# A scan with a gated feed-forward on one core: an earlier load of h, and the first two down products exchanged

## The chip, the cores and the metric

The kernel runs on one core of a Trainium2 chip. The time is the device time of one execution in microseconds (us), the median over several runs. One more execution was taken with the hardware profiler; its views (waits, timelines, windows) are what the prediction reads. The engines of a core are called by short names: PE is TensorE (matrix products, with its weight loads as PEld), DVE is VectorE, ACT is ScalarE, POOL is GpSimd, and SP issues most DMA transfers. Each engine works through its own list of instructions in the order in which the program gives them; an instruction that waits holds back all that stand behind it on the same engine.

## The reference

```python
def reference(A_x, A_wqkv, A_wo, B_x, B_w_gate, B_w_up, B_w_down):
    ...
    x = A_x
    xn = _layernorm(x, axis=-1)
    s = _A_ref(xn, A_wqkv, A_wo)
    g = _silu(_B_ref(xn, B_w_gate, B_w_up, B_w_down))
    return x + s * g
```

`x` has 2048 rows of 640. `_A_ref` is attention of 32 heads over 8 earlier rows, each two apart, with a product by `wo` (640 x 640) at its end. `_B_ref` is `((x W_gate) * (x W_up)) W_down`, with 1536 columns in the middle. All is float32.

## The kernel before

**The whole.** The 2048 rows make 16 tiles of 128. The kernel has three stages for TensorE: the products with `wqkv`, `w_gate` and `w_up`, beside the attention on the other engines; then the output product with `wo` for pairs of tiles (`pair_product`, L981); then the down product with `w_down` for pairs of tiles (`product`, L853). The middle result h (the gated product) and the attention's output go through DRAM: `h_scr` holds h, tile by tile, and `s_scr` the output of `wo`.

**Float32 in two parts.** Every operand of a matmul is split into a high part (a copy to the type fp32r, on ACT) and a low part (the operand less its high part, on DVE or POOL), and each product is three: high by high, high by low, low by high, in this order. So an operand costs one ACT instruction and one DVE or POOL instruction before TensorE can use it. For h these are `hi_h(m)` (L820, ACT at L822) and `lo_h(m)` (L824, DVE at L826); for a pair of the `wo` stage `hi_pair` and `lo_pair` (L968, L972); for weights `split_wd` (L781), whose helper `split` (L112) runs ACT at L114 and POOL at L115.

**Seven products for a pair.** A pair of tiles, seen as a 2 x 2 matrix of blocks A11 to A22, is multiplied with the 2 x 2 blocks of the weight in seven block products instead of eight, by sums of blocks. The seven left operands are, in order, A11, S1, S2, S4, S3, A12 and A22 (`H_IN`, L731), and the right ones B11, T1, T2, B22, T3, B21 and T4 (`W_IN`). For h the sums are made by `sum_h` (L803) on DVE: S1 = A21 - A22 (L810), S2 = S1 - A11 (L812), S4 = A12 + S2 (L815), S3 = A11 - A21 (L818; it is written in the place of A21). S1 needs the second tile of the pair alone, S2 needs S1 and the first tile.

**Banks.** The products add into three PSUM banks, and which product uses which is the string `"ACACABA"` (L856): product 0 starts bank A, product 1 bank C, product 2 adds into A, product 3 into C, product 4 into A, product 5 starts bank B, product 6 adds into A. `gather(m)` (L866) follows each product. For product 0 it is `keep("M1")`, for product 1 `keep("M5")`, for product 2 `keep("U2")`: a copy of the bank by ACT (L840), which must be done before the next product adds into that bank.

**The border.** The loop over pairs p = 0 to 7 (L1490) makes the seven products of pair p, and between them prepares pair p + 1; the first product of pair p + 1 stands before the last product of pair p. In its last rounds it prepares the down stage too, all in an order written out by hand:

- at the start of p = 6, `load_h(0, (1,))` loads the second tile of h's first pair (768 KB, L795 on SP); after product 4 of p = 6, `load_h(0, (0,))` loads the first. Each takes the buffer (tag `t`, two buffers) of an earlier pair of the `wo` stage and waits for `lo_pair` of that pair;
- in p = 7, `sum_h(1)` (S1) stands after product 1, `hi_h(1)`, `lo_h(1)` and `hi_h(0)` after product 2, `lo_h(0)` after product 4, and `sum_h(2)` (S2) after product 5;
- behind the loop stand two splits of T4 weights, the loads for later (`load_h(1)`, `load_sx`), then `hi_h(2)`, `sum_h(3)` (S4) and `lo_h(2)`.

In the copies of a pair's products, ACT at L999 and L1010 and DVE at L1002 to L1007, TensorE's banks are read; L1010 is the copy after product 6.

**The down stage.** Its loop over m runs four products ahead (`AHEAD`): behind product m and `gather(m)` stand `hi_h(m + 4)` on ACT, then the sum for m + 5 and `lo_h(m + 4)` on DVE. At m = 0 there stand first `hi_h(3)`, `sum_h(4)` (S3) and `lo_h(3)`. So on ACT the order is: the copy of the first product, `hi_h(3)`, `hi_h(4)`, the copy of the second product, and so on; `hi_h(4)` needs S3.

Of the kernel before, what the change touches and what calls it, by code (L numbers as in the profile page):

```python
# [42 lines left out]
NP = NT // 2  # L43
# [13 lines left out]
def kernel(  # L57
# [70 lines left out]
    def slot(shape, dt=F32R):  # L128
        return st(shape, "s", SLOTS, dt)
# [651 lines left out]
    def split_wd(u):  # L781

        n = sum(len(ks) for _, ks in u)
        y, r = w_row[u[0][0], u[0][1][0]]
        split(nc.gpsimd, wd_raw.pop(u), *(y[:, r:r + n, l] for l in range(2)))
# [3 lines left out]
    def load_h(n, rows=(0, 1)):  # L789

        v = h_raw.setdefault(n, {})
        if n % 2 == 0:
            for i in rows:
                t = st([P, KF, P], "t", 2)
                nc.sync.dma_start(t, h_scr[2 * n + i])  # L795
                v.update({f"A{i + 1}1": t[:, :KH], f"A{i + 1}2": t[:, KH:]})
        else:
            for name, i, k, tag, m in (("A11", 0, 0, "wraw", 2), ("A21", 1, 0, "s", SLOTS), ("A12", 0, KH, "o", 1),
                                       ("A22", 1, KH, "wraw", 2)):
                v[name] = st([P, KH, P], tag, m)  # L800
                nc.sync.dma_start(v[name], h_scr[2 * n + i][:, k:k + KH])

    def sum_h(m):  # L803

        n, name = m // 7, H_IN[m % 7]
        v = h_raw[n]
        if name == "S1":
            y = slot([P, 2, KH, P], F32)
            v["S1"], v["S2"] = y[:, 0], y[:, 1]
            nc.vector.tensor_sub(v["S1"], v["A21"], v["A22"])  # L810
        elif name == "S2":
            nc.vector.tensor_sub(v["S2"], v["S1"], v["A11"])  # L812
        elif name == "S4":
            v["S4"] = slot([P, KH, P], F32)
            nc.vector.tensor_add(v["S4"], v["A12"], v["S2"])  # L815
        elif name == "S3":
            v["S3"] = v["A21"]
            nc.vector.tensor_sub(v["S3"], v["A11"], v["A21"])  # L818

    def hi_h(m):  # L820
        hT[m] = slot([P, 2, KH, P])
        nc.scalar.activation(hT[m][:, 0], h_raw[m // 7][H_IN[m % 7]], AF.Copy)  # L822

    def lo_h(m):  # L824
        n, name = m // 7, H_IN[m % 7]
        nc.vector.tensor_sub(hT[m][:, 1], h_raw[n][name], hT[m][:, 0].bitcast(F32))  # L826
        if name == "A22" and n + 2 < NT // 2:
            load_h(n + 2)
# [24 lines left out]
    def product(m):  # L853
        j = m % 7
        name = W_IN[j]
        place = "ACACABA"[j]  # L856
        new = j in (0, 1, 5)
        if new:
            bank[place] = pt([P, HALF], {"A": "q", "B": "g", "C": "u"}[place], {"A": 3, "B": 2, "C": 2}[place])
        p, y = bank[place], hT.pop(m)  # L860
        runs = [(i, l, k) for i, l in ((0, 0), (0, 1), (1, 0)) for k in range(KH)]
        for r, (i, l, k) in enumerate(runs):
            nc.tensor.matmul(p, y[:, i, k], wd_part(name, k, l), start=new and r == 0, stop=r == len(runs) - 1,  # L863
                             skip_group_check=True)

    def gather(m):  # L866

        n, j = divmod(m, 7)
        a, b = 2 * n, 2 * n + 1
        p = bank["ACACABA"[j]]  # L870
        if j == 0:
            keep("M1", p, "lg", 2)
        elif j == 1:
            keep("M5", p, "lg", 2)
        elif j == 2:
            keep("U2", p, "gh", 5)
        elif j == 3:
            g_t[a] = slot([P, D], F32)
            nc.vector.tensor_sub(g_t[a][:, HALF:], p, kept["U2"])
            return lambda: silu(a, 1)  # L880
        elif j == 4:
            g_t[b] = slot([P, D], F32)
            nc.vector.tensor_sub(g_t[b][:, HALF:], kept["M5"], p)
            return lambda: silu(b, 1)
        elif j == 5:
            nc.vector.tensor_add(g_t[a][:, :HALF], kept["M1"], p)
            return lambda: silu(a, 0)
        else:
            return lambda: silu(b, 0, p)
        return lambda: None  # L890
# [90 lines left out]
    def pair_product(p, j):  # L981
        place = "ACACABA"[j]
        new = j in (0, 1, 5)
        if new:
            bank[p, place] = pt([P, HALF], {"A": "q", "B": "g", "C": "u"}[place], {"A": 3, "B": 2, "C": 2}[place])
        b = bank[p, place]
        runs = [(pair_in(p, H_IN[j], k, i), w_part(W_IN[j], k, l)) for i, l in ALL3 for k in range(KS)]
        if j in FIFTH:
            name, c = FIFTH[j]
            runs += [(pair_in(p, name, 0, i), wo_t["W0-W1"][:, l] if c is None else wo_s[KD - 1][l][:, c:c + HALF])  # L990
                     for i, l in ALL3]
        for r, (y, w) in enumerate(runs):
            nc.tensor.matmul(b, y, w, start=new and r == 0, stop=r == len(runs) - 1, skip_group_check=True)  # L993
        if j == 0:
            pair_first[p] = st([P, HALF], "lg", 2)
        kept = [pair_first[p]] + [pair_k[0][:, i] for i in range(2)]
        ya, yb = y_t.setdefault((p, "y"), [None, None])
        if j < 3:
            nc.scalar.activation(kept[j], b, AF.Copy)  # L999
        elif j == 3:  # L1000
            ya = y_t[p, "y"][0] = st([P, D], "gh", 5)
            nc.vector.tensor_add(ya[:, HALF:], kept[2], b)  # L1002
        elif j == 4:
            yb = y_t[p, "y"][1] = st([P, D], "gh", 5)
            nc.vector.tensor_add(yb[:, HALF:], kept[1], b)
        elif j == 5:
            nc.vector.tensor_add(ya[:, :HALF], kept[0], b)  # L1007
            nc.sync.dma_start(s_scr[2 * p], ya)
        else:
            nc.scalar.activation(yb[:, :HALF], b, AF.Copy)  # L1010
            nc.sync.dma_start(s_scr[2 * p + 1], yb)
# [339 lines left out]
    for m, t in ((m, t) for m in range(1, len(MADE)) for t in range(DIL)):  # L1351
# [3 lines left out]
        for i in range(NE):  # L1355
            n = t * NE + i
# [92 lines left out]
    def unit(name, *ks):  # L1449
        return ((name, ks),)  # L1450
# [32 lines left out]
    def low_then_split(p, part, n):  # L1483
        lo_pair(p, part)
        behind(pair_z[p, part][0][1][:, KD - 1, P - 1:].bitcast(F32))
        split_next(n)
# [3 lines left out]
    for p in range(NP):  # L1490
        more = p + 1 < NP
        if p:
            wd_loads()
        if p == NP - 2:
            load_h(0, (1,))
        elif not more:
            load_wd((unit("T3", 4, 5), unit("T4", 2, 3)), "pk", 1)
            load_wd((unit("T4", 4, 5),), "gh", 5)
        pair_product(p, 1)
        if more:  # L1500
            hi_pair(p + 1, 0)
            low_then_split(p + 1, 0, 1)
        else:
            split_next()
            sum_h(1)
        pair_product(p, 2)
        if more:
            hi_pair(p + 1, 2)
        else:
            hi_h(1)  # L1510
            lo_h(1)
            hi_h(0)
        pair_product(p, 3)
        if more:
            hi_pair(p + 1, 1)
        else:
            split_next(2)
        pair_product(p, 4)
        if more:
            lo_pair(p + 1, 2)  # L1520
            if p == NP - 2:
                load_h(0, (0,))
        else:
            lo_h(0)
        pair_product(p, 5)
        if not more:
            sum_h(2)
            split_wd(unit("T3", 4, 5))
        if more:
            low_then_split(p + 1, 1, 2 if p in (5, 6) else 1)  # L1530
        if p == 0:
            load_pair(4)
        elif p > 1 and p + 3 < NP:
            load_pair(p + 3)
        if p + 2 < NP:
            turn_pair(p + 2)
        if more:
            pair_product(p + 1, 0)
        pair_product(p, 6)
    split_wd(unit("T4", 4, 5))  # L1540
    split_wd(unit("T4", 2, 3))
    load_h(1)
# [5 lines left out]
    lo_h(2)  # L1548
    for m in range(n_prod):
        n, j = divmod(m, 7)  # L1550
        product(m)
        after = gather(m)
        if m == 0:
            hi_h(AHEAD - 1)
            sum_h(AHEAD)
            lo_h(AHEAD - 1)
        if m + AHEAD < n_prod:
            hi_h(m + AHEAD)
        after()
        if m + AHEAD + 1 < n_prod:  # L1560
            sum_h(m + AHEAD + 1)
        if m + AHEAD < n_prod:
            lo_h(m + AHEAD)
        if j < 2 and n:
            gated(2 * n - 2 + j)
            load_sx(2 * n + j)
        if m == n_prod - 3:
            gated(NT - 2, HALF)
            gated(NT - 1, HALF)
        elif m == n_prod - 2:  # L1570
            gated(NT - 2, 0)
# [44 lines left out]
```

## Time and profile before

| | |
|---|---|
| Median of 3 runs | 742.34 us (741.77 to 743.74) |
| The profiled execution, its own time | 741.97 us |
| Its span, from the first to the last event of the core | 740.1 us |
| Down stage, its first product's start | 586.03 us from the start of the span |
| Mean granted TensorE clock | 0.999 |

A row of a timeline gives the start and the length in us, the engine, the line of the kernel, the operation, the tiles it writes and reads (without buffer numbers), the shapes, and a count where several instructions in a row are merged. In square brackets stands the idle time of the engine just before it and what ended that. In a row of waits the three numbers are the total, how often, and the longest. The tiles of this border: `t` are h's two tiles of the first pair and the pairs' raw data, `s` are operands and sums, `q`, `e`, `u` and `g` are PSUM banks (bank A is a `q` or an `e`, bank C is a `u`, bank B is a `g`), `lg` is where `keep` copies the first two products to, `xc` and `kv` hold split weights, and `wraw`, `pk` and `gh` hold weights as they were loaded.

### The profile page before, as it was taken

Reading aid. Unit: us, or ns where it says so; the run is one execution under the profiler, and the core shown is the slowest. Engines: PE = TensorE matmul, PEld = TensorE weight load, DVE = VectorE, ACT = ScalarE, POOL = GpSimd, SP = SyncE. Lnnn points to the kernel's source line nnn. Section 1 sums busy time; section 2 is a strip of 40 time slices with the busy share of each in tenths; the row PEclk is TensorE's granted clock in tenths of the full one; section 3 lists DMA queues with packets and bytes.
Section 4 is the critical chain, followed back from the end, with each engine's and each line's share of the span. In section 5 each row is a group of like instructions: output and inputs, shape, how many; then the busy total and the mean of one; then the engine's idle time right before and its main releaser. Section 6 shows DMA issues by size and latency. Waiting matters only on the chain.

```text
span 740.1 us, 11057 instructions
## 1 busy us (share of the span) xinstructions
PE 730.8 (99%) x4030; PEld 665.4 (90%) x4030; DVE 625.9 (85%) x729; ACT 301.4 (41%) x560; POOL 448.4 (61%) x382
## 2 busy tenths in 40 slices
PE   8999999999999999999999999999999999999997
PEld 6989989988999998887878888888999999999997
DVE  7676998799786989899989999968888887777775
ACT  5668312323232333233323332335556654444442
POOL 6159929997788889797879969577543720000000
PEclk9999999999999999999999999999999999999999
DMA  9465588889767659452634443268667855555534
GB/s 331 160 203 166 218 281 301 249 255 256 190 183 190 228 163 362 120 188 60 205 92 118 158 141 91 74 199 224 204 213 231 305 203 192 192 192 193 193 107 142
DMA packets 106292, 143.78 MB, mean 194 GB/s; under 512 B 23064, under 2 KB 75284, under 8 KB 106238
## 3 DMA queue, kind: packets, MB, share of 16 engines
q1 hardware_dynamic: 88510, 121.13, 51.3%
q10 hardware_dynamic: 16000, 12.78, 5.4%
q0 software_dynamic: 1728, 9.18, 5.3%
q8 instruction: 31, 0.51, 0.3%
q14 instruction: 23, 0.19, 0.1%
HBM read 94.40 MB, written 55.67 MB: 203 GB/s over the span
## 4 chain that ended last, share of the span: by engine, by line
PE 92%; POOL 2%; DVE 2%; issue 2%; DMA 1%; ACT 1%; SPq 0%; POOLq 0%; DVEq 0%; ACTq 0%
PE g L1289 14%; PE q L434 10%; PE u L1289 9%; PE u L434 8%; PE q L863 8%; PE g L434 8%; PE u L863 5%; PE g L124 5%; PE u L124 5%; PE q L1289 4%; PE q L993 3%; PE e L863 3%; PE g L863 3%; PE u L993 2%; PE e L434 1%
## 5 line engine op out<-in xcount | busy, mean ns | idle before, releaser
L514 POOL TENSOR_TENSOR o<-o,t 128x960 f32<-128x960 f32 (+1 forms) x66 | 132.9, 2014 | 9.5 <-DVE t L508 8.5
L508 DVE TENSOR_TENSOR t<-e,kv 128x960 f32<-128x960 f32 (+1 forms) x96 | 99.6, 1038 | 16.7 <-POOL o L514 16.7
L542 DVE TENSOR_TENSOR t<-q,kv 128x1920 f32<-128x1920 f32 (+1 forms) x48 | 92.5, 1926 | 2.9 <-DMA kv<-qkv_scr 1.9
L549 DVE TENSOR_REDUCE lg<-t 128x96 f32<-128x1920 f32 (+1 forms) x48 | 92.3, 1923 | 0.2
L434 PE MATMUL q<-s,xc 128*128 128x360 f32 (+1 forms) x450 | 82.9, 334 | 0.2 <-POOL s L115 0.2
L1258 ACT ACTIVATE gh<-g 128x512 f32<-128x512 f32 x57 | 34.1, 599 | 113.1 <-PE g L1289 109.4
L115 POOL TENSOR_TENSOR s<-wraw,s 128x384 fp32r<-128x384 f32 (+6 forms) x57 | 69.5, 1231 | 17.6 <-ACT s L114 17.6
L434 PEld LDWEIGHTS q<-s,xc 128*128 128x128 f32 x450 | 74.8, 188 | 4.3 <-POOL s L115 1.3
L434 PE MATMUL u<-s,xc 128*128 128x360 f32 (+1 forms) x360 | 65.8, 334 | 0.0
L434 PEld LDWEIGHTS u<-s,xc 128*128 128x128 f32 x360 | 60.3, 188 | 2.3
L434 PE MATMUL g<-s,xc 128*128 128x360 f32 (+1 forms) x330 | 61.5, 337 | 0.0
L1289 PE MATMUL u<-xc,s 128*128 128x512 f32 x228 | 58.1, 390 | 0.3 <-POOL s L115 0.3
L1289 PE MATMUL g<-s,s 128*128 128x512 f32 x228 | 58.0, 390 | 0.2 <-ACT gh L1258 0.2
L434 PEld LDWEIGHTS g<-s,xc 128*128 128x128 f32 x330 | 55.7, 188 | 2.6
L863 PE MATMUL q<-xc,s 128*128 128x320 f32 x342 | 55.5, 309 | 0.0
L863 PEld LDWEIGHTS q<-xc,s 128*128 128x128 f32 x342 | 51.5, 188 | 0.0
L1289 PEld LDWEIGHTS u<-xc,s 128*128 128x128 f32 x228 | 42.8, 188 | 9.6 <-POOL s L115 0.8
L1289 PEld LDWEIGHTS g<-s,s 128*128 128x128 f32 x228 | 42.7, 188 | 9.5 <-ACT gh L1258 0.6
L114 ACT ACTIVATE s<-wraw 128x384 fp32r<-128x384 f32 (+6 forms) x58 | 32.6, 581 | 29.8 <-PE g L1289 10.2
L1289 PE MATMUL g<-xc,s 128*128 128x512 f32 x171 | 42.0, 390 | 0.1
L1289 PE MATMUL q<-xc,pk 128*128 128x512 f32 x171 | 41.9, 389 | 0.0
L826 DVE TENSOR_TENSOR s<-s,s 128x768 fp32r<-128x768 f32 x28 | 30.5, 1088 | 11.8 <-ACT s L822 11.8
(332 smaller groups left out, 1547.0 us busy)
## 6 DMA issues: line engine op xcount, KB each, us to landing
h_scr<-gh SPq DMA_DIRECT2D x48, 256.0 KB, 2.6
wraw<-in_wgu SPq DMA_DIRECT2D x11, 640.0 KB, 4.4
kv<-qkv_scr SPq DMA_DIRECT2D x14, 480.0 KB, 6.0
t<-h_scr SPq DMA_DIRECT2D x8, 768.0 KB, 5.9
qkv_scr<-s ACTq DMA_DIRECT2D x17, 360.0 KB, 4.3
kv<-qkv_scr SPq DMA_DIRECT2D x14, 367.5 KB, 6.8
s_scr<-gh SPq DMA_DIRECT2D x16, 320.0 KB, 3.3
gh<-s_scr SPq DMA_DIRECT2D x16, 320.0 KB, 4.1
```

Source lines behind the costliest of these rows:

```text
L114: nc.scalar.activation(hi, raw, AF.Copy)
L115: eng.tensor_sub(lo, raw, hi.bitcast(F32))
L124: nc.tensor.matmul(acc, a, b, start=first and n == 0, stop=last and n == len(runs) - 1)
L434: nc.tensor.matmul(p, xT[(r * NE + i) // TPC][a][:, k, t0:t0 + P], wq[m][b][k], start=n == 0, stop=n == len(runs) - 1, skip_group_check=ac ...
L508: nc.vector.tensor_mul(t.rearrange("p (n d) -> p n d", d=DH), e[:, :, w].unsqueeze(2).to_broadcast([P, NE * nh, DH]), v)
L514: return NE * c * cost, lambda: eng.tensor_add(y, z, t)
L542: nc.vector.tensor_mul(t, q, k)
L549: nc.vector.tensor_reduce(out=lg[:, :, j:j + 2].rearrange("p n a -> p a n"), in_=t.rearrange("p a (n d) -> p a n d", d=DH), op=ALU.add, ax ...
L863: nc.tensor.matmul(p, y[:, i, k], wd_part(name, k, l), start=new and r == 0, stop=r == len(runs) - 1, skip_group_check=True)
L993: nc.tensor.matmul(b, y, w, start=new and r == 0, stop=r == len(runs) - 1, skip_group_check=True)
L1258: nc.scalar.activation(kept[j], b["ACACABA"[j]], AF.Copy)
L1289: nc.tensor.matmul(y, w, x, start=j in (0, 1, 5) and r == 0, stop=r == len(runs) - 1, skip_group_check=True)
```

## The change

Four things are moved in the border, and none is added or left out:

- `load_h(0, (1,))`, the load of h's second tile, goes from the start of p = 6 to p = 5, after product 4 and `lo_pair(6, 2)`;
- `sum_h(1)` (S1) goes from p = 7, after product 1, to the end of p = 6, behind the last `lo_pair` of pair 7;
- `hi_h(0)`, `lo_h(0)` and `sum_h(2)` (S2) go from p = 7 to behind the loop, in front of the two T4 splits;
- the down loop's first two products change places, with their `gather`: the order of the first seven is 1, 0, 2, 3, 4, 5, 6.

```diff
@@ -1491,9 +1491,7 @@
         more = p + 1 < NP
         if p:
             wd_loads()
-        if p == NP - 2:
-            load_h(0, (1,))
-        elif not more:
+        if not more:
             load_wd((unit("T3", 4, 5), unit("T4", 2, 3)), "pk", 1)
             load_wd((unit("T4", 4, 5),), "gh", 5)
         pair_product(p, 1)
@@ -1502,14 +1500,12 @@
             low_then_split(p + 1, 0, 1)
         else:
             split_next()
-            sum_h(1)
         pair_product(p, 2)
         if more:
             hi_pair(p + 1, 2)
         else:
             hi_h(1)
             lo_h(1)
-            hi_h(0)
         pair_product(p, 3)
         if more:
             hi_pair(p + 1, 1)
@@ -1518,16 +1514,15 @@
         pair_product(p, 4)
         if more:
             lo_pair(p + 1, 2)
-            if p == NP - 2:
-                load_h(0, (0,))
-        else:
-            lo_h(0)
+            if p >= NP - 3:
+                load_h(0, (NP - 2 - p,))
         pair_product(p, 5)
-        if not more:
-            sum_h(2)
-            split_wd(unit("T3", 4, 5))
         if more:
             low_then_split(p + 1, 1, 2 if p in (5, 6) else 1)
+        else:
+            split_wd(unit("T3", 4, 5))
+        if p == NP - 2:
+            sum_h(1)
         if p == 0:
             load_pair(4)
         elif p > 1 and p + 3 < NP:
@@ -1537,6 +1532,9 @@
         if more:
             pair_product(p + 1, 0)
         pair_product(p, 6)
+    hi_h(0)
+    lo_h(0)
+    sum_h(2)
     split_wd(unit("T4", 4, 5))
     split_wd(unit("T4", 2, 3))
     load_h(1)
@@ -1548,8 +1546,8 @@
     lo_h(2)
     for m in range(n_prod):
         n, j = divmod(m, 7)
-        product(m)
-        after = gather(m)
+        product(m if n else (1, 0, 2, 3, 4, 5, 6)[m])
+        after = gather(m if n else (1, 0, 2, 3, 4, 5, 6)[m])
         if m == 0:
             hi_h(AHEAD - 1)
             sum_h(AHEAD)
```

## The prediction

> **What bounds the kernel now.** I read the page's busy shares first, then the waits of TensorE, then the timeline of the border between the last pair (p = 7) and the down products. The page:
>
> ```profile
> PE 730.8 (99%) x4030; PEld 665.4 (90%) x4030; DVE 625.9 (85%) x729; ACT 301.4 (41%) x560; POOL 448.4 (61%) x382
> ```
>
> TensorE (PE) works for 730.8 of 740.1 us. Whatever delays it is added to the time, and the border can give back no more than its idle time there. The waits, and the timeline of TensorE (start, length, engine, line, out<-in, count, idle time in front and what ended it):
>
> ```profile
> PE u L863 <- ACT lg L840: 1.6, 1, 1.6
> PE e L993 <- DVE gh L1005: 0.6, 1, 0.6
> ```
>
> ```profile
> 584.62 1.14 PE L993 MATMUL e<-xc,s 128*128 128x320 f32 x6 [0.64 <-DVE gh L1005]
> 586.03 2.80 PE L863 MATMUL q<-xc,s 128*128 128x320 f32 x18
> 588.67 2.80 PE L863 MATMUL u<-xc,s 128*128 128x320 f32 x18
> 591.31 0.90 PE L863 MATMUL q<-kv,s 128*128 128x320 f32 x5
> 595.68 0.99 PE L863 MATMUL u<-kv,s 128*128 128x320 f32 x5 [1.57 <-ACT lg L840]
> ```
>
> Products 0, 1 and 2 start at 586.03, 588.67 and 591.31: 2.64 us each, 0.147 per matmul. Product 3 waits 1.57 us, because it adds into the bank of product 1, which ScalarE (ACT) must copy out first (`keep("M5")`, L840). So the border holds 0.64 + 1.57 = 2.2 us of idle time, 0.3% of the span: the most that the change can gain, and about what a measurement of this kernel can tell from no change.
>
> Why was that copy late? ACT, VectorE (DVE) and GpSimd (POOL):
>
> ```profile
> 584.21 0.74 ACT L114 ACTIVATE xc<-wraw 128x640 fp32r<-128x640 f32 x1 [1.54 <-DMA wraw<-in_wd]
> 587.01 0.42 ACT L1010 ACTIVATE gh<-e 128x320 f32<-128x320 f32 x1
> 588.12 0.74 ACT L114 ACTIVATE xc<-gh 128x640 fp32r<-128x640 f32 x1 [0.69 <-DMA gh<-w_scr]
> 589.39 0.83 ACT L822 ACTIVATE s<-s 128x768 fp32r<-128x768 f32 x1
> 590.45 0.83 ACT L822 ACTIVATE s<-s 128x768 fp32r<-128x768 f32 x1
> 594.46 0.84 ACT L822 ACTIVATE s<-t 128x768 fp32r<-128x768 f32 x1 [3.19 <-DVE t L818]
> 595.21 0.42 ACT L840 ACTIVATE lg<-u 128x320 f32<-128x320 f32 x1
> ```
>
> ```profile
> 584.48 0.95 DVE L826 TENSOR_TENSOR s<-t,s 128x768 fp32r<-128x768 f32 x1
> 585.75 1.93 DVE L812 TENSOR_TENSOR s<-s,t 128x768 f32<-128x768 f32 x1
> 587.71 2.22 DVE L815 TENSOR_TENSOR s<-t,s 128x768 f32<-128x768 f32 x1
> 590.25 1.93 DVE L826 TENSOR_TENSOR s<-s,s 128x768 fp32r<-128x768 f32 x1 [0.32 <-ACT s L822]
> 592.11 2.32 DVE L818 TENSOR_TENSOR t<-t,t 128x768 f32<-128x768 f32 x1
> 599.58 0.94 DVE L810 TENSOR_TENSOR s<-s,wraw 128x768 f32<-128x768 f32 x1
> ```
>
> ```profile
> 561.29 1.58 POOL L115 TENSOR_TENSOR kv<-wraw,kv 128x640 fp32r<-128x640 f32 x1
> 585.03 4.09 POOL L115 TENSOR_TENSOR xc<-wraw,xc 128x640 fp32r<-128x640 f32 x2 [2.08 <-ACT xc L114]
> 589.08 2.29 POOL L115 TENSOR_TENSOR xc<-pk,xc 128x640 fp32r<-128x640 f32 x1
> 591.34 2.28 POOL L115 TENSOR_TENSOR xc<-gh,xc 128x640 fp32r<-128x640 f32 x1
> 593.57 2.25 POOL L115 TENSOR_TENSOR xc<-pk,xc 128x640 fp32r<-128x640 f32 x1
> ```
>
> ACT stood 3.19 us before `hi_h(4)` (594.46) for S3, which DVE ended at 594.43; `keep("M5")` was queued behind it. DVE ran, in order, `lo_h(0)`, S2, S4, `lo_h(2)`, S3. Its 128x768 operations take 0.94 alone (the row at 599.58), but about 2 here, and the ends say why: POOL 589.12, S4 589.93, POOL 591.37, `lo_h(2)` 592.18, POOL 593.62, S3 594.43. They alternate, 0.81 for DVE and 1.44 for POOL: what reads two SBUF tiles on the one waits for the other's instruction to end. From the end of `lo_h(0)`, 585.43, four POOL and four DVE operations give 4 x 1.44 + 4 x 0.81 = 9.0, or 594.43, as measured. This serial sum sets the border, and it begins when the first B21 weights land (ACT's wait for `in_wd` in front of 584.21, then POOL's for ACT in front of 585.03).
>
> **The change, part by part.**
>
> *The load and the sum S1*, with the timeline of DVE and of the DMA queue of SP:
>
> ```profile
> 567.03 0.95 DVE L972 TENSOR_TENSOR s<-t,s 128x768 fp32r<-128x768 f32 x1
> 568.47 0.32 SPq L1008 DMA_DIRECT2D s_scr<-gh  x1
> 572.06 4.41 SPq L795 DMA_DIRECT2D t<-h_scr  x2
> 576.49 0.82 DVE L972 TENSOR_TENSOR s<-s,s 128x640 fp32r<-128x640 f32 x1
> 577.93 2.04 DVE L810 TENSOR_TENSOR s<-t 128x768 f32<-128x768 f32 x1 [0.61 <-DMA t<-h_scr]
> ```
>
> Two windows (length, busy time of each engine, granted clock, share of the DMA engines, GB/s):
>
> ```profile
> 568.00:572.00 4.00, 4.00 (x29) 4.00 (x28) 3.90 (x7) 1.80 (x4) 1.86 (x3) 1.00 0.39 145
> 572.00:586.00 14.00, 13.36 (x90) 12.87 (x89) 11.05 (x15) 8.75 (x16) 8.19 (x7) 1.00 0.95 326
> ```
>
> The load waits for `lo_pair(6, 2)`, the last reader of its buffer, which ends at 567.98; it goes out about 568.0 instead of 572.06, past two stores and two weight loads on SP. The first store starts at 568.47 anyway: nothing is held up. DVE's order does not change by moving S1, since it had no other work between L972 at 576.49 and S1; only the 0.61 us wait goes. `hi_h(1)` stays behind the copy after product 2, so this is worth nothing by itself. What it may bring is in the two windows: the 768 KB move out of a stretch that is 0.95 busy into one that is 0.39 busy, so the B21 weights may land sooner. Bounds: 0, and 1.8 us, the overlap of the two h loads (the second goes out with the end of the x2 row less one issue, 576.15; the first lands at 577.93). The stretch keeps the other h load, which still goes out at 576.15 behind `lo_pair(7, 2)`, and all the weights, so I take 0.4, nearer to 0.
>
> *The 0.64 us in front of (7,6).* `lo_h(1)` stands where it stood; whether it now gets in front of a POOL split is open. Either way (gain 0 to 0.64) it is swallowed below, since a wait for the serial sum comes after.
>
> *`hi_h(0)`, `lo_h(0)` and S2 behind the last pair.* `hi_h(0)` now stands on ACT behind L1010, which ends at 587.43; with 0.84 it ends at 588.2. Behind it on ACT are the two T4 splits (the first waits for its DMA until 588.12 anyway) and `hi_h(2)`; behind `lo_h(0)` on DVE are S2, S4, `lo_h(2)` and S3. DVE, which did `lo_h(0)` at 584.48 and S2 at 585.75, now stands idle to 588.2. POOL uses that time: its first two splits run alone, 585.03 + 2 x 1.58 = 588.19. From there three POOL splits (1.44 each) and `lo_h(0)`, S2, S4 (0.81 each) alternate to 588.19 + 4.32 + 2.43 = 594.94. With POOL done, `lo_h(2)` and S3 take 0.87 each (0.94 less the 0.07 by which the row at 592.11 starts before the end of the one in front of it): 596.7. Before, S3 ended at 594.43: 2.2 us of the idle stretch are lost.
>
> *The exchange of products 0 and 1.* Product 1 takes 586.03, product 0 588.67, with `hi_h(0)` ready at 588.2 and `lo_h(0)` by 590.43, when its last six matmuls want it. Product 0 ends its turn at 591.31. Now product 2 comes next, and it adds into the bank of product 0, so it waits for `keep("M1")`, with no product in between. On ACT that copy is queued behind `hi_h(4)`, which waits for S3. From S3's end to TensorE's start took 595.68 - 594.43 = 1.25 us; so product 2 starts at 596.7 + 1.25 = 597.9 rather than 591.3. The new wait is 6.6, and the 1.57 in front of product 3 goes (its copy is now ahead). Net +5.0, or +4.6 with weights 0.4 sooner, +3.2 with 1.8. Nothing later takes it back: TensorE has no wait after 595.68 in the list.
>
> *The clock after so long a wait.* No row shows TensorE idle for 6 us within the work; the two ends of the span come nearest:
>
> ```profile
> 1.35 1.65 PE L229 MATMUL q<-lg 128*128 128x384 f32 x2 [1.35 <-POOL lg masks.py:199]
> 2.79 1.49 PE L229 MATMUL e<-lg 128*128 128x384 f32 x2
> 4.08 1.55 PE L229 MATMUL q<-lg 128*128 128x384 f32 x4
> 16.77 0.60 PE L313 MATMUL g<-lg,t 128*128 128x128 f32 x4
> 17.21 0.27 PE L313 MATMUL e<-lg,t 128*128 128x128 f32 x1
> ```
>
> ```profile
> 733.00:736.00 3.00, 2.87 (x20) 2.60 (x18) 1.48 (x3) 0.57 (x2) 0.00 (x0) 1.00 0.28 101
> 738.00:740.10 2.10, 0.00 (x0) 0.00 (x0) 0.00 (x0) 0.00 (x0) 0.00 (x0) 0.73 0.21 78
> ```
>
> The last matmul ends at 735.87 (2.87 of that window are busy), and the granted clock (third column from the end) is 0.73 over 738.0 to 740.1: half speed from about 739.0, after 3.1 us of idleness. At the start two 128x384 matmuls take 1.29 us (2.79 to 4.08), 1.68 ns a column; four of 128 columns take 0.44 later (16.77 to 17.21), 0.86 ns a column. So TensorE starts at half speed, and the x4 row, with two fast ones in it, ends at 5.63: full speed came after some 3.4 to 4.3 us of work. My wait of 6.2 (6.6 less 0.4) is twice the 3.1. Half speed for 3.8 us then costs 1.9 us. Bounds: 0, if the clock holds, and 3.8, if the slow stretch is twice as long. I take 1.9, by the row at the start. [...]
>
> Sum: +4.6 + 1.9 = +6.5. On the profiled execution (741.97) (a span of 740.1 and 1.9 around it) that is 748.5; on the median of the runs (742.34, 0.37 above it) 748.8.
>
> **The rivals.**
>
> *The clock holds.* Same chain, no slow stretch: +3.2 to +5.0, about 747.0. For it: the windows above with work in them show 1.00, the 0.64 us wait among them. Against it: the new wait is four times as long as the longest in the list.
>
> *Faster: the exchange does what product 3 needs.* `keep("M5")` is then no longer last, and product 2 waits only for product 0's end and its own copy, about 0.5 (0.42 and handing over): 0.64 + 1.57 - 0.5 = 1.7 gained, 740.6. It decides at 590.1: S3 must end by then (1.25 before 591.31). Against it: from the end of `hi_h(0)` alone, 588.2, five DVE operations take 4 us even with no POOL.
>
> *No change.* The load moves and the sum waits as before, because the weights, landing sooner, pull the whole border forward: the serial sum would have to begin 5 us sooner, almost three times the most that I allow the weights. Time 742.3.
>
> **How the numbers follow.** Wait and slow clock 0.60; wait with the clock held 0.28; no change 0.06; faster 0.04, and at -1.7 it lies mostly within 0.3%; a smaller wait, +1 to +2.2, 0.02. The predicted time is the first's, 748.8. The range runs from the second case's low end (+3.2, 745.5) to the first's high end (5.0 + 3.8, 751.1). Faster by over 0.3% (2.2 us): 0.02; within: 0.10; slower: 0.88.
>
> **What would show it.** Right: in the waits of TensorE a row for L863 on `q` behind ACT L840 of some 6 us, none on `u`; DVE idle in front of L826 `s<-t,s` until about 589, behind ACT L822; S3 (L818) ending near 596.5; granted clock under 1 after the wait. S1 without its DMA wait. Wrong: product 2 starting within 1 us of product 0's end, or S3 ending before 592.

## The result, and the profile after

The changed kernel takes 749.62 us (749.06 to 749.83, 5 runs) against 743.0 for the kernel before (741.77 to 744.77, 5 runs): a ratio of 1.0086 (95% interval 1.0069 to 1.0103), slower by 6.6 us. Single executions of the kernel before differ by a few us among themselves (739.9 to 745.4 on the chip of the first four experiments), and with the granted clock, the share of full speed that TensorE was given: of the 66 taken beside the experiments, the 27 with a mean of 0.999 or 1.000 have a median of 741.8 us, the 24 with 0.997 or less one of 744.1. So steps of the border are compared inside one trace, from a mark that all kernels have: the start of the last `lo_pair` of pair 7 on VectorE (L972, 128x640; 576.49 in the trace of before). From there to the start of product 3 it is 19.19 us in the kernel before and 26.51 in the changed one, 7.3 more.

The waits of TensorE in the changed kernel (total, times, longest):

```profile
PE q L863 <- ACT lg L840: 6.2, 1, 6.2
PE e L993 <- DVE gh L1005: 0.5, 1, 0.5
PE q L863 <- ACT s L822: 0.2, 1, 0.2
```

The 1.6 us on bank `u` are gone, and there are 6.2 on bank `q`, behind the same copy line. The timeline of the changed kernel's border, with VectorE, GpSimd, ScalarE and TensorE picked out:

```profile
576.91 0.82 DVE L972 TENSOR_TENSOR s<-s,s 128x640 fp32r<-128x640 f32 x1
586.62 0.74 ACT L114 ACTIVATE xc<-wraw 128x640 fp32r<-128x640 f32 x1 [1.80 <-DMA wraw<-in_wd]
588.15 0.42 ACT L1010 ACTIVATE gh<-e 128x320 f32<-128x320 f32 x1
588.46 0.83 ACT L822 ACTIVATE s<-t 128x768 fp32r<-128x768 f32 x1
588.97 1.57 POOL L115 TENSOR_TENSOR xc<-pk,xc 128x640 fp32r<-128x640 f32 x1
589.33 2.02 DVE L826 TENSOR_TENSOR s<-t,s 128x768 fp32r<-128x768 f32 x1 [4.09 <-ACT s L822]
589.35 3.20 PE L863 MATMUL q<-xc,s 128*128 128x320 f32 x18 [0.22 <-ACT s L822]
590.49 2.27 POOL L115 TENSOR_TENSOR xc<-gh,xc 128x640 fp32r<-128x640 f32 x1
591.27 2.31 DVE L812 TENSOR_TENSOR s<-s,t 128x768 f32<-128x768 f32 x1
592.73 2.25 POOL L115 TENSOR_TENSOR xc<-pk,xc 128x640 fp32r<-128x640 f32 x1
593.62 2.17 DVE L815 TENSOR_TENSOR s<-t,s 128x768 f32<-128x768 f32 x1
596.58 0.94 DVE L818 TENSOR_TENSOR t<-t,t 128x768 f32<-128x768 f32 x1
597.56 0.84 ACT L822 ACTIVATE s<-t 128x768 fp32r<-128x768 f32 x1 [0.89 <-DVE t L818]
598.31 0.42 ACT L840 ACTIVATE lg<-q 128x320 f32<-128x320 f32 x1
598.78 1.70 PE L863 MATMUL q<-kv,s 128*128 128x320 f32 x5 [6.23 <-ACT lg L840]
603.42 0.90 PE L863 MATMUL u<-kv,s 128*128 128x320 f32 x5
```

The first row is the mark. Read the rest from the bottom. Product 2 (598.78) waited 6.23 us for `keep("M1")` (598.31), which stood on ScalarE behind `hi_h(4)` (597.56), which waited for S3 (596.58 to 597.5). S3 was late because VectorE stood idle for 4.09 us in front of `lo_h(0)` and then took turns with GpSimd's splits: 2.02, 2.31 and 2.17 us for operations of 0.94. And product 2 takes 598.78 to 603.42, 4.64 us rather than 2.64. The windows (length, busy times, granted clock, share of the DMA engines, GB/s) say why:

```profile
594.00:596.00 2.00, 0.00 (x0) 0.00 (x0) 2.00 (x2) 1.01 (x3) 0.97 (x1) 1.00 1.02 401
596.00:598.00 2.00, 0.00 (x0) 0.00 (x0) 2.00 (x3) 1.11 (x2) 0.00 (x0) 0.55 1.03 405
598.00:600.00 2.00, 1.22 (x4) 1.22 (x5) 1.86 (x3) 1.46 (x3) 0.00 (x0) 0.50 0.24 96
600.00:602.00 2.00, 2.00 (x9) 2.00 (x9) 0.46 (x1) 0.00 (x0) 0.00 (x0) 0.50 0.28 31
602.00:604.00 2.00, 2.00 (x12) 2.00 (x11) 0.00 (x0) 0.33 (x1) 0.00 (x0) 0.74 0.90 350
```

The granted clock is at half from about 596.2 to about 603.0 (0.55 of one window, 0.74 of the last): 6.8 us, of which 4.2 have work in them.

The whole move of product 3, from 595.68 to 603.42, is 7.74: the border starts 0.30 later in this execution, product 0 starts 0.38 late (it waits for `hi_h(0)`) and lasts 0.40 longer (it waits for `lo_h(0)`), 6.23 of waiting, 2.00 of slow clock, less the 1.57 of before.

### The profile page after: what moved, and what is told of

Its sections match the earlier page's. It is cut to its first block, busy times and chain, and to the rows that moved or that the text cites. A ratio compares the mean times of both kernels' runs of the same rounds, so it can differ in the third digit from the quotient of the medians.

```text
span 747.8 us, 11058 instructions
## 1 busy us (share of the span) xinstructions
PE 733.8 (98%) x4030; PEld 667.2 (89%) x4030; DVE 622.1 (83%) x729; ACT 301.8 (40%) x560; POOL 446.8 (60%) x382
## 5 line engine op out<-in xcount | busy, mean ns | idle before, releaser
L508 DVE TENSOR_TENSOR t<-e,kv 128x960 f32<-128x960 f32 (+1 forms) x96 | 99.4, 1036 | 16.2 <-POOL o L514 16.2
L514 POOL TENSOR_TENSOR o<-t 128x960 f32<-128x960 f32 (+1 forms) x11 | 22.2, 2017 | 28.5 <-DVE t L508 24.5
```

Of the source, the lines that this page charges most:

```text
L508: nc.vector.tensor_mul(t.rearrange("p (n d) -> p n d", d=DH), e[:, :, w].unsqueeze(2).to_broadcast([P, NE * nh, DH]), v)
L514: return NE * c * cost, lambda: eng.tensor_add(y, z, t)
```

## The experiments

My theory: the loss is a wait for the copy of product 0, which stands on ScalarE behind `hi_h(4)` and so behind S3; S3 is late, since VectorE's chain starts late and alternates with GpSimd; and TensorE's clock fell to 0.50 during the wait. The rivals: the late operands of product 0 alone, the exchange alone, or something in the DMA traffic. Ratios are to runs of the kernel before on the same chip.

| run | us | ratio (95% interval) | mark to product 3 |
|---|---|---|---|
| before | 743.0 | | 19.19 |
| changed | 749.62 | 1.0086 (1.0069 to 1.0103) | 26.51 |
| no exchange | 743.83 | 1.0013 (1.0001 to 1.0025) | 21.56 |
| exchange only | 746.86 | 1.0056 (1.0042 to 1.0070) | 25.25 |
| early load and S1 only | 743.87 | 1.0010 (0.9995 to 1.0025) | 19.07 |
| late `hi_h(0)`, `lo_h(0)`, S2 only | 743.46 | 1.0007 (0.9994 to 1.0019) | 21.82 |
| copies first | 744.57 | 1.0024 (1.0012 to 1.0036) | 22.33 |
| kept warm | 746.41 | 1.0045 (1.0029 to 1.0062) | 24.31 |
| splits held | 743.11 | 1.0006 (0.9993 to 1.0019) | 21.66 |
| both waits | 740.90 | 0.9966 (0.9954 to 0.9979) | 16.56 |
| both waits, buffer free | 739.47 | 0.9939 (0.9917 to 0.9960) | 16.56 |

### Without the exchange

```diff
-        product(m if n else (1, 0, 2, 3, 4, 5, 6)[m])
-        after = gather(m if n else (1, 0, 2, 3, 4, 5, 6)[m])
+        product(m)
+        after = gather(m)
```

> The changed kernel, but with the first two down products in their old order 0, 1, 2. My theory (the copy of product 0 stands on ScalarE behind hi_h(4), which waits for S3; the exchange puts product 2 directly behind that copy; then the halved clock): S3 still ends near 597.5, but TensorE has products 0, 1 and 2 to do until then, so it waits in pieces of at most 3 us (some 3 in front of product 0, for hi_h(0), and 1 to 2 in front of product 3), product 3 starts near 598.5, the clock stays full: about +2.8 on the kernel before, 745.8, near 4 us less than the changed kernel. Rival (the late hi_h(0), lo_h(0) and S2 alone make the loss, the exchange does nothing): no difference from the changed kernel, 749.6. Second rival (the exchange alone makes the loss): back at 743.0.

It took 743.83, 1.0 us over the kernel before by the ratio, where 2.8 was expected. Most of the loss goes with the exchange, so the first rival falls; the size was off, and by the time alone the second rival, 743.0, is the nearer one. The trace shows what is left: 21.56 from the mark to product 3 against 19.19. Timeline and windows of this run:

```profile
587.68 4.45 PE L863 MATMUL q<-xc,s 128*128 128x320 f32 x18 [2.41 <-ACT s L822]
596.67 0.42 ACT L840 ACTIVATE lg<-u 128x320 f32<-128x320 f32 x1
597.25 0.90 PE L863 MATMUL u<-kv,s 128*128 128x320 f32 x5
```

```profile
585.00:588.00 3.00, 0.59 (x4) 0.33 (x4) 0.34 (x1) 2.88 (x5) 2.40 (x3) 1.00 0.70 278
588.00:591.50 3.50, 3.50 (x15) 3.50 (x14) 3.50 (x2) 0.88 (x2) 3.50 (x3) 0.51 0.98 298
```

TensorE waited in front of product 0 as expected (2.41), but behind it no more: the copy (596.67) was done before product 3 wanted to start at 597.25. What I had not expected is the second window: the clock was 0.51 after a wait of 2.41 us, and product 0 took 4.45. The mean clock of the 12 executions ran from 0.994 to 0.999, so not every one pays the same for this.

### The exchange only

```diff
 (the kernel before)
-        product(m)
-        after = gather(m)
+        product(m if n else (1, 0, 2, 3, 4, 5, 6)[m])
+        after = gather(m if n else (1, 0, 2, 3, 4, 5, 6)[m])
```

> The kernel before with nothing but the exchange of the first two down products. [...] Rival (the late hi_h(0) alone makes the loss): 743.0. Rival that the exchange helps as it is meant to: 741.

I had expected 745.8, by a wait of 4.4 us in front of product 2 in place of the 1.6 in front of product 3, and up to 747.8 if the clock halved too. It took 746.86, a ratio of 1.0056, between the two cases. The clock is 0.50 in two windows of the profiled execution (747.69), and the mean clock is 0.994 or 0.995 in all six (timeline, then windows):

```profile
595.98 0.42 ACT L840 ACTIVATE lg<-q 128x320 f32<-128x320 f32 x1
596.45 1.70 PE L863 MATMUL q<-kv,s 128*128 128x320 f32 x5 [5.31 <-ACT lg L840]
```

```profile
594.80:598.20 3.40, 1.75 (x6) 1.75 (x7) 3.18 (x4) 1.90 (x3) 0.00 (x0) 0.50 0.75 293
598.20:601.60 3.40, 3.40 (x14) 3.40 (x14) 0.00 (x0) 0.00 (x0) 0.00 (x0) 0.50 0.62 215
```

Nothing but the exchange, and the wait of 5.31 for `keep("M1")` is there. So the exchange alone makes most of the loss: it puts product 2 directly behind the copy that it needs, while in the order 0, 1, 2 product 2's bank is copied during product 1 and only product 3 can be caught. What the late `hi_h(0)` adds is the later S3.

### The early load and S1 only

```diff
 (the kernel before)
-        if p == NP - 2:
-            load_h(0, (1,))
...
-            sum_h(1)
...
-            if p == NP - 2:
-                load_h(0, (0,))
+            if p >= NP - 3:
+                load_h(0, (NP - 2 - p,))
...
+        if p == NP - 2:
+            sum_h(1)
```

> The kernel before with nothing but the earlier load of h's second tile and S1 at the end of p = 6; hi_h(0), lo_h(0), S2 and the products as before. As predicted, the emptier DMA queues bring the B21 weights up to 1.8 us sooner: 0 to -1.8, I took 0.4 (742.6). A rival read from the changed kernel's trace: S1, no longer waiting for its DMA, runs in front of GpSimd's first split, that split ends 1.0 us later, the B21 weights are asked for 1.0 us later because that split frees their buffer, and so the border is 0 to 1 us later: up to 744.0; then the issue of the in_wd loads moves from 579.2 to about 580.2.

The ratio of 1.0010 (0.9995 to 1.0025) can't be told from no change, and from the mark to product 3 it is 19.07 against 19.19. The queue of SP and three other rows of this run:

```profile
577.16 0.95 DVE L810 TENSOR_TENSOR s<-t 128x768 f32<-128x768 f32 x1
577.38 0.78 POOL L186 COPY beside<-s 128x1 f32<-128x1 f32 x1 [2.16 <-DVE s L972]
579.71 0.89 SPq L778 DMA_DIRECT2D wraw<-in_wd  x2
583.53 0.74 ACT L114 ACTIVATE xc<-wraw 128x640 fp32r<-128x640 f32 x1 [1.48 <-DMA wraw<-in_wd]
```

S1 runs without its wait and at 0.95 rather than 2.04, but in front of GpSimd, whose small copy now takes 0.78 where it took 0.18; the split behind it frees the buffer of the next weights later, and these go out 3.3 us after the mark instead of 2.7. SP's queue waits 0.6 us for GpSimd in front of them, a wait that the trace of before does not have. So the rival's step is there, with 0.6 us rather than 1.0. The first of the weights is in use 7.10 after the mark (583.53) instead of 7.72 (584.21), in spite of that. That the emptier DMA queues do this is not shown: in the four other runs with the load at its old place it is 6.8 to 8.3. At product 3 nothing is left of either.

### The late hi_h(0), lo_h(0) and S2 only

```diff
 (the kernel before)
             lo_h(1)
-            hi_h(0)
...
-        else:
-            lo_h(0)
...
-            sum_h(2)
...
         pair_product(p, 6)
+    hi_h(0)
+    lo_h(0)
+    sum_h(2)
```

> The kernel before with nothing but hi_h(0), lo_h(0) and S2 moved behind the last pair; load, S1 and the order of the products as before. My theory: much like the run without the exchange: TensorE waits some 2.5 us in front of product 0 and little behind it; from the last lo_pair of pair 7 to the start of product 3 it takes 1 to 2.5 us more than the kernel before, up to 1.8 of it by the clock: 743.5 to 745.5. Rival (the early load and S1 do something of their own here): it differs from the run without the exchange by more than 1 us.

743.46, a ratio of 1.0007, and 21.82 from the mark to product 3 against 21.56 without the exchange: the early load does nothing of its own here either. Product 0 takes 4.44 us here, after a wait of 2.14; without the exchange it took 4.45, at a clock of 0.51, so the clock seems to have halved here too (no window of this run shows it):

```profile
587.10 4.44 PE L863 MATMUL q<-xc,s 128*128 128x320 f32 x18 [2.14 <-ACT s L822]
```

So the parts alone measure +0.56% (exchange), +0.07% (late operands) and +0.10% (load), the last two not to be told from 0; these add up to 0.73%, and the whole change measures +0.86%. In the traces the late operands alone do cost 2.6 us up to product 3. With the exchange they cost by way of S3: it ends 20.6 us after the mark in the changed kernel and 19.0 in the run with the exchange only, and product 2 starts 1.6 later with it.

### Both copies in front of hi_h(3)

```diff
 (the changed kernel)
+        if m == 0:
+            for i in (1, 0):
+                product(i)
+                gather(i)
+        if m < 2:
+            after = lambda: None
+        else:
+            product(m)
+            after = gather(m)
```

> The changed kernel with the copies of products 1 and 0 both in front of hi_h(3) and hi_h(4) on ScalarE; TensorE's and VectorE's order is unchanged. My theory: the copy of product 0 now waits only for hi_h(2) (near 594.5) instead of hi_h(4), product 2 starts near 595.3 instead of 598.8, the wait is under 3.1 us, the clock stays full, product 3 starts near 598.0 instead of 603.4: 744.2, +1.2 on the kernel before. Rival (the operands, not the copy's place, hold product 2): no change from 749.6. Rival (place matters but not the clock): 746.2, the 2 us of a slow product 2 staying.

744.57, by the ratios 0.6% or 4.6 us less than the changed kernel, by moving the copy of product 0, 0.42 us long, forward in ScalarE's queue: its place there is shown to make most of the wait. Two rows of the timeline, and two windows:

```profile
594.25 1.11 PE L863 MATMUL q<-kv,s 128*128 128x320 f32 x5 [2.45 <-ACT lg L840]
598.52 0.91 PE L863 MATMUL u<-kv,s 128*128 128x320 f32 x5
```

```profile
591.50:594.90 3.40, 0.95 (x6) 0.68 (x6) 3.37 (x3) 1.54 (x4) 2.51 (x2) 1.00 0.98 325
594.90:598.30 3.40, 3.40 (x15) 3.40 (x14) 3.36 (x4) 2.38 (x3) 0.00 (x0) 0.51 0.98 382
```

The wait is 2.45, now behind `hi_h(2)`, and product 2 still takes 4.27 (594.25 to 598.52): I had expected a full clock. It was 0.51 after a stretch in which TensorE worked for 0.95 of 3.40 us. The 744.2 expected is near the 744.57 measured although it left this slow stretch out.

### TensorE kept at work during the wait

```diff
 (the changed kernel)
+        if m == 1:
+            fill(0, "B11", 36)
         if m == 0:
             hi_h(AHEAD - 1)
```

The function `fill`, which is not shown, multiplies product 0's high part by the weights once more, into a bank `g`.

> The changed kernel with 36 more matmuls of 128x320 between product 0 and product 2, into a bank that nobody reads: extra work, which TensorE does while it waits for the copy of product 0 (36 x 0.147 = 5.3 us of the 6.2). My theory (about 2.0 us of the loss is product 2 at the halved clock, 4.64 instead of 2.64): the wait shrinks to about 1 us, the clock stays full, product 2 takes 2.64 and starts where it did: 2.0 less than the changed kernel, 747.6. Rival (the clock costs nothing, the slow product 2 has another cause, such as its operands): 749.6, and product 2 still takes 4.6.

Timeline (the lines are ten further down here: L859 is the fill, L873 `product`) and one window:

```profile
590.79 5.44 PE L859 MATMUL g<-xc,s 128*128 128x320 f32 x36
596.88 1.00 PE L873 MATMUL q<-kv,s 128*128 128x320 f32 x5 [0.64 <-ACT lg L840]
599.62 0.90 PE L873 MATMUL u<-kv,s 128*128 128x320 f32 x5
```

```profile
596.00:600.00 4.00, 3.36 (x23) 3.13 (x22) 2.41 (x3) 1.69 (x4) 0.00 (x0) 1.00 0.48 177
```

With 5.4 us of useless work more, the kernel is faster: 746.41 against 749.62. Product 2 takes 2.74 (596.88 to 599.62) at a clock of 1.00, 1.9 less than in the changed kernel: the slow product 2 was the clock. From the mark to product 3 it is 24.31 instead of 26.51, 2.2 less, since product 2 also starts 0.3 sooner here. The times differ by 3.2, more than the 2.0 expected; in the two traces 1.6 us of the difference lie in front of the mark, where the kernels are the same.

### GpSimd's splits held behind S3

```diff
 (the changed kernel: the T3 and T4 splits move)
+        if m == 1:
+            behind(h_raw[0]["S3"][:, KH - 1, P - 1:])
+            split_wd(unit("T3", 4, 5))
+            split_wd(unit("T4", 4, 5))
+            split_wd(unit("T4", 2, 3))
+            load_sx(0)
+            load_sx(1)
```

`behind(y)` is a copy of one element a partition on GpSimd that reads `y`, so that what stands behind it there waits for `y`. ScalarE's halves of the three splits and the two `load_sx` move along.

> The changed kernel with GpSimd's last three splits (T3 and the two of T4) held back until S3 is done; GpSimd's work is moved, not left out. My theory (VectorE's chain to S3 is long because it alternates with those three splits, 1.44 each): lo_h(0), S2, S4, lo_h(2) and S3 run at 0.9 each from about 589.0, S3 ends near 593.4 instead of 597.5, product 2 starts near 594.7 instead of 598.8, the wait is 2.3 instead of 6.2, product 3 starts between 597.3 (clock full) and 599 (one window at half clock): 743.5 to 745.2. Rival (the chain is set by ScalarE or by data, not by GpSimd): S3 stays near 597.5 and the time at 749.6.

```profile
588.63 0.95 DVE L812 TENSOR_TENSOR s<-s,t 128x768 f32<-128x768 f32 x1
589.61 0.96 DVE L815 TENSOR_TENSOR s<-t,s 128x768 f32<-128x768 f32 x1
591.42 0.95 DVE L818 TENSOR_TENSOR t<-t,t 128x768 f32<-128x768 f32 x1
593.63 1.70 PE L863 MATMUL q<-kv,s 128*128 128x320 f32 x5 [2.62 <-ACT lg L840]
```

743.11, a ratio of 1.0006, a little under the range that was expected. (The 1.7 us between its ends are an estimate for a slow clock; in the run with the copies first product 2 took 1.63 longer, 4.27 instead of 2.64.) S2 and S4 take 0.95 instead of 2.31 and 2.17, S3 ends 16.2 us after the mark instead of 20.6, and the wait shrinks from 6.23 to 2.62. Of the 4.4 us by which S3 is sooner, 3.2 are VectorE's chain (from the end of `hi_h(0)` to that of S3 it is 5.1 instead of 8.2): it was long because of GpSimd. The other 1.2 are `hi_h(0)`, which ends sooner: ScalarE's half of the T3 split no longer stands in front of it, and the second B21 weights came 0.35 sooner. The clock halves in this trace too: it is 0.50 from 594.0 to 596.0 and 1.00 again from 598.0 to 600.0, and product 2 takes 4.17 us (593.63 to 597.80).

### The two waits of the kernel before, and a version that beats both

```diff
 (the kernel before)
-            split_next()
...
             lo_h(1)
+            behind(hT[1][:, 1, KH - 1, P - 1:].bitcast(F32))
+            split_next()
...
-    split_wd(unit("T4", 4, 5))
-    split_wd(unit("T4", 2, 3))
...
-        product(m)
-        after = gather(m)
+        if m != 1:
+            product(m)
+            after = gather(m)
...
             lo_h(AHEAD - 1)
+            behind(hT[AHEAD - 1][:, 1, KH - 1, P - 1:].bitcast(F32))
+            split_wd(unit("T4", 4, 5))
+            split_wd(unit("T4", 2, 3))
+            product(1)
+            gather(1)
```

`split_next()` makes the next split of weights, here a T3 one. The two `load_sx` move with the T4 splits.

> Not the change, but the kernel before with the two waits of its border attacked: the copy of product 1 stands in front of hi_h(4), the two T4 splits are held behind lo_h(3), and the last T3 split behind lo_h(1). My theory (both waits are queue places behind VectorE operations that alternate with GpSimd's splits): the wait of 0.6 in front of (7,6) and that of 1.6 in front of product 3 both go, 2.2 us, 0.3%: 740.9. Rival (another operand is late next, so that nothing is gained): 743.1, with a new wait of 1 to 2 us at product 3 or 4. It should beat both kernels if the theory holds.

740.90, a ratio of 0.9966 (0.9954 to 0.9979), as expected in size, though the rival was half right. The two old waits are gone (product 3 starts 16.56 after the mark instead of 19.19), and there is a new one, in the waits of TensorE and of ScalarE:

```profile
PE q L863 <- ACT gh L840: 1.4, 1, 1.4
```

```profile
ACT gh L840 <- POOL xc L115: 2.6, 1, 2.6
```

The copy of product 2 needed a `gh` buffer, and the T4 split that I had held back still read one. The next run holds T3 in its place, with the loads back where they were:

```diff
 (the run above)
-            split_wd(unit("T3", 4, 5))
...
+    split_wd(unit("T4", 4, 5))
...
-            split_wd(unit("T4", 4, 5))
+            split_wd(unit("T3", 4, 5))
             split_wd(unit("T4", 2, 3))
```

> As the run that attacks both waits of the kernel before, but of the three last splits it is the first T4 split that runs at its old place, and T3 and the second T4 split that are held behind lo_h(3). My theory for the new wait there (1.4 us in front of product 4: the copy of product 2 waited 2.6 for a gh buffer, which the held T4 split still read): no split that reads a gh buffer is held, so the copy of product 2 starts on time, no wait over 0.3 us is left at the border, product 4 starts 1.4 sooner, and the down stage ends some 2.4 us sooner than in the kernel before: 740.5, 0.5 to 1 under that run if one could tell. Rival (product 4 waits for T3, now split later, or for hi_h(4)): a wait of 1 us or more stays in front of product 4.

739.47 (738.63 to 739.59), a ratio of 0.9939 (0.9917 to 0.9960): 0.6% faster than the kernel before. TensorE's list of waits has none in the border any more; two windows of it, the products 0 to 4 (584.87 to 598.07) but for their first 1.1 us:

```profile
586.00:592.00 6.00, 6.00 (x43) 6.00 (x42) 5.97 (x4) 4.22 (x7) 4.60 (x3) 1.00 0.89 316
592.00:598.00 6.00, 6.00 (x43) 6.00 (x42) 5.95 (x7) 4.94 (x7) 4.41 (x3) 1.00 0.99 369
```

From the mark to the end of the span it is 161.2 us against 163.7 in the trace of before (162.6 in the run above): 2.4 less, as expected. By the ratio it gains 4.6. The record speaks for the clock as the rest: on this chip three of the 12 executions of the kernel before have a mean clock of 0.999 or 1.000 and take 740.3 to 742.7, and the nine with 0.995 to 0.998 take 743.7 to 745.6, while all seven of this run have 0.998 or more. In the run above it is 0.999 or 1.000 in all eight, against 12 of 25 for the kernel before. My estimate from these counts is that the border's waits cost the kernel before its full clock in half of its executions or more; no trace of such an execution was taken, so it is not shown where the clock falls in them.

## Why the prediction was right

Forecast: +6.5; measured: +6.6. That the two are so close is in part luck: by the two profiled executions it is +7.8, and the medians differ by less because that of the kernel before (743.0) holds executions slower than the profiled one (741.97). By its steps:

- **The wait for `keep("M1")` behind `hi_h(4)` and S3.** Forecast 6.6, 6.2 with the weights sooner; measured 6.23, on the bank and behind the instruction that were named. The size agrees because both of its ends moved: S3 and the end of product 0 came about 1 us later than forecast. Shown by moving the copy (4.6 us less) and by the exchange alone, which makes the wait without the rest.
- **S3 near 596.5.** Measured 597.5. The forecast took the turns of VectorE and GpSimd from the moment when `hi_h(0)` ends, which it set at 588.2; it was 589.3, for the second B21 weights came late. That the rest of the chain is turns with GpSimd is shown by holding GpSimd back: 3.2 us less from the end of `hi_h(0)` on.
- **The weights 0.4 sooner.** The term of the sum that was mis-sized. The first weights came 0.6 us sooner, the second later (ScalarE began on them 586.62, 9.71 us after the mark, instead of 9.06). The forecast said that the earlier S1 was worth nothing by itself; it has a price, since it now runs in front of GpSimd's split, and that split frees the buffer of these weights. How much of the 0.65 it is stays open: the second weights come 8.8 to 9.4 after the mark in the five other runs with the early load, and 8.3 to 9.1 in the four with the load at its old place.
- **Product 0 without a stall.** The margin of 0.5 us for `hi_h(0)`, and the one of nothing for `lo_h(0)`, did not hold: 0.38 and 0.40. This makes most of the 0.9 us by which the sum was short in the trace, where product 3 moved by 7.74 - 0.30.
- **The clock, 1.9 us.** Measured 2.00 in the trace, and 1.9 by the run that keeps TensorE at work (product 2 in 2.74 instead of 4.64). The rival in which the clock holds falls. The half speed lasted 6.8 us, where the forecast took 3.8, but product 2 began 2.6 us into it, so the price was near that of the 3.8: luck, since the forecast let the half speed begin with product 2. No run shows a slow stretch of 3.8 (it was about 3.4 us in the run with the copies first). Nor can the row at the start of the span carry the 3.8: listed by shape, two of the four matmuls merged in its x4 row are 128x128, so they are short and not fast, and L313, with which it was compared, is transposes. The clock records of the same trace begin at full speed 5.1 us into the span, 3.7 us after the first matmul; what the clock was before that, they do not show.
- **The rival on the other side,** that product 2 waits for nothing but its own copy, would have needed S3 by 590.1; it came 7 us later. With the copies first the exchange still lost 0.24%; whether it can gain once no copy waits was not run. The last two runs remove the waits with the old order.

## What to carry to other kernels

An evacuation that a later product waits for should not stand in an engine's queue behind work that waits for another engine: here moving one 0.42 us copy was worth 4.6 us. Before products change places, look which product adds into the bank of the one directly in front of it: the distance between the two is the time that the copy has, here the 2.64 us of product 1 before the exchange, and none after it. And work that is moved to a later place is priced by what it then takes turns with, not by its own length: S2 and S4 took 2.31 and 2.17 us beside GpSimd's splits, and 0.95 and 0.96 with these held back.

## What the runs showed of the hardware that was not expected

- TensorE's clock halved after much shorter waits than the 3.1 us that the end of the span suggested: it was 0.51 after 2.45 us in the run with the copies first, where TensorE had worked for 0.95 us of the 3.40 in front of it, and 0.51 after 2.41 in the run without the exchange; in the run with the late operands only, the 4.44 us of product 0 speak for the same after 2.14. After the waits of 0.6 and 1.6 in the profile of before it was 1.00.
- It did not come back at once with work: in the run with the exchange only, a stretch of 3.40 us with 1.75 of work in it (594.8 to 598.2) stayed at 0.50, and so did a second one, full of work; only after both, 6.8 us, was it 1.00 again. In the run with the copies first one stretch of 3.4, full of work, was enough: 0.51 in it, 0.98 in the 1.7 us behind it.
- Even GpSimd's copy of one element a partition took 0.78 us instead of 0.18, once S1 ran on VectorE in front of it. In the run with the early load it ends at 578.16, and S1 at 578.11.
